# Splitting the output block of the paired units around the state

## The chip, the cores and the metric

The kernel runs on one core of a Trainium2 chip. The metric is the device time of the program in microseconds (us), measured on the chip; every launch gives one time. A profile of one launch comes with each measurement.

## The reference, cut to what matters

The reference is a retention layer (attention with a decay per head instead of a softmax) followed by a two-layer network with a squared ReLU.

```python
# q, k, v: (8, 8, 576, 64); w_in: (512, 2048); w_out: (2048, 512)
scores = scale * np.matmul(q, k.transpose(0, 1, 3, 2))
Dmat = np.where(rel >= 0, gamma[:, None, None] ** rel[None, :, :], 0.0)
attn = np.matmul(scores * Dmat, v)
x = attn.transpose(0, 2, 1, 3).reshape(4608, 512)
h = x @ w_in
g = np.maximum(h, 0.0) ** 2
out = g @ w_out
```

The decay allows the retention to be done in chunks of 128 positions. A chunk's output is a part inside the chunk (masked scores times v) plus a part from the state R, the decayed sum of k times v of all chunks before.

## The kernel before

The work is cut in 36 units (128 tokens each) in 18 groups of two. In a group, TensorE (PE) makes the scores and sums, VectorE (DVE) applies the mask and updates R, PE makes the output psO, VectorE scales it to xT, and then come the big products: ph (xT times w_in), a squared ReLU to gT, and po (gT times w_out). Groups 1 to 4 take the "paired" path, which this change is about. The other 14 groups have their own code and use a product scheme with sums such as gS and wT (VectorE sums of gT pieces and of w_out pieces).

The instructions of each engine are put in order at build time. Every task is added with an engine, a priority key, an assumed duration and its dependencies, and a small simulation of the engines pops the ready task with the lowest key. So a changed key or dependency can move other instructions too.

The paired path, with cuts marked by "...":

```python
def add_ret_pair(g):
    ...
    def fr1(s=s, src=src):     # psS + R of the unit before
        nc.vector.tensor_tensor(out=r, in0=rT["sum"][s][:, 0:256], in1=tile_of["R", src], op=ALU.add)
    def fr2(s=s, src=src):     # times the decay: the new R, two inputs from SBUF (stmp and dec)
        nc.vector.tensor_tensor(out=r..., in0=x..., in1=dec128..., op=ALU.mult)
    ...
    def inter(other):          # the part of the states, 8 small products (4 without a carried state)
        for n in range(2):
            for a, b in ((0, 0), (1, 1), (0, 1), (1, 0)):
                s = a ^ other
                if s or carry:
                    x = 2 * n + b
                    put2(s, 4 * n + 2 * a + b, tile_of["R", u + s - 1][half(a), half(x)], kqT(s)[half(a), NP + x, :], a)
    def fo():
        tile_of["psO", g] = ps_ret.tile([P, 2, 512], FP32, name="psO", tag="prO")
        inter(1)
        nc.tensor.drain()
        for m in range(NP):    # the part that needs no state, 32 small products of rx and vx
            ...
        inter(0)
    t = add("PE", base + 24, 1.3, fo, deps=masked + [T["R", u]] + ([T["R", u - 1]] if carry else []), acq=("prO",))
```

The whole output block waits for the masks and for R together. Each weight quarter is cast from a staging buffer in two halves, one on GpSimd (POOL) and one on ScalarE (ACT):

```python
def fc(eng=eng, rows=rows, sl=sl):
    (nc.gpsimd.tensor_copy if eng == "POOL" else nc.scalar.copy)(out=dst[:, rows, sl], in_=s[:, rows, sl])
```

In all later units GpSimd also multiplies v by its decay, one instruction of 128x512 per unit:

```python
def fv():
    t = tile_of["v16", u] = cast.tile([P, H, D], FP16, name="v16", tag="v16")
    nc.gpsimd.tensor_tensor(out=t, in0=tile_of["v32", u],
        in1=vdec[kind].rearrange("p (h o) -> p h o", o=1).to_broadcast([P, H, D]), op=ALU.mult)
```

Of the kernel before, what the change touches and what calls it, by code (L numbers as in the profile page):

```python
# [15 lines left out]
class Schedule:  # L16
# [7 lines left out]
    def add(self, eng, key, dur, fn, deps=(), acq=(), after=None, lag=0.0):  # L24
        t = dict(eng=eng, key=key, dur=dur, fn=fn, acq=acq, n=len(self.tasks), users=[], free=[], lag=lag,
                 left=len(deps), ready=0.0, lat=self.LAT[eng] if after is None else after)
        for d in deps:
            d["users"].append(t)
        self.tasks.append(t)
        return t  # L30
# [73 lines left out]
def kernel(  # L104
# [9 lines left out]
    nc = tc.nc  # L114
# [102 lines left out]
    for hp in range(NP):  # L217
# [18 lines left out]
                          R=6, Rm=6, kqT=6))  # L236
    add = sched.add
# [99 lines left out]
    T = {}  # L337
# [4 lines left out]
    def quad(out_, lhsT, rhs, row, col, start=True):  # L342
        nc.tensor.matmul(out_, lhsT=lhsT, rhs=rhs, start=start, stop=True, skip_group_check=True,  # L343
                         tile_position=(64 * row, 64 * col))

    def half(x):
        return slice(64 * x, 64 * x + 64)
# [90 lines left out]
    def add_ret_pair(g):  # L438

        u = groups[g][0]  # L440
        base = base_of(g)
        carry = units[u][2] > 0
        kqT = lambda s: tile_of["kqT", u + s]
        masked = []
        rT = {}
        for e in range(2):
            tag = "prS" if e == 0 else "prO"

            def fs(e=e, tag=tag):
                ps = rT["ps", e] = ps_ret.tile([P, 2, 512], FP32, name="psc", tag=tag)  # L450
                for hp in range(NP):
                    for a, s in ((0, 0), (1, 1), (0, 1), (1, 0)):
                        quad(ps[half(s), a, hp * P:(hp + 1) * P], kqT(s)[half(a), hp, half(e)], kqT(s)[half(a), NP + hp, :],
                             a, s)
            t = add("PE", base + 3 + e, 0.4, fs, deps=T["kqT", u] + T["kqT", u + 1], acq=(tag,))
            ms = []
            for a in range(2):
                def fm(e=e, a=a):
                    if a == 0:
                        rT[e] = cast.tile([P, 2, NP, P], FP16, name="rx", tag="kq16")  # L460
                    nc.vector.tensor_tensor(
                        out=rT[e][:, a], in0=rT["ps", e][:, a].rearrange("p (n i) -> p n i", i=P),
                        in1=mask2[:, e].rearrange("p (o e) i -> p o (e i)", o=1).to_broadcast([P, NP, P]), op=ALU.mult)
                ms.append(add("DVE", base + 5 + e, 0.66, fm, deps=[t] + ms, acq=() if a else ("kq",)))
            sched.free(tag, ms)
            masked += ms

        def fk():
            ps = rT["sum"] = [ps_ff.tile([P, 512], FP32, name="psS", tag="ff") for s in range(2)]
            for hp in range(NP):  # L470
                for e in range(2):
                    for s, a in ((0, 0), (1, 1), (0, 1), (1, 0)):
                        h = 4 * (hp // 2) + 2 * a + hp % 2
                        quad(ps[s][half(a), 64 * hp:64 * hp + 64], tile_of["kx", u][half(s), e, 128 * hp + 64 * a:128 * hp + 64 * a + 64],
                             tile_of["vx", u][half(s), e, 64 * h:64 * h + 64], s, a, start=hp == 0 and e == 0)
        t = add("PE", base + 4.5, 0.5, fk, deps=T["kvx", u], acq=("ff", "ff"))
        sched.free("kq", [t])
        chain = []
        for s in range(2):
            src = None if s == 0 and not carry else u + s - 1  # L480

            def fr1(s=s, src=src):
                r = tile_of["tmp", u + s] = work.tile([P, NP * D], FP32, name="stmp", tag="stmp", bufs=1)
                nc.vector.tensor_tensor(out=r, in0=rT["sum"][s][:, 0:256], in1=tile_of["R", src], op=ALU.add)

            def fr2(s=s, src=src):
                r = tile_of["R", u + s] = st_pool.tile([P, NP * D], FP16, name="R", tag="R")
                x = rT["sum"][s][:, 0:256] if src is None else tile_of["tmp", u + s]
                nc.vector.tensor_tensor(
                    out=r.rearrange("p (n d) -> p n d", d=D), in0=x.rearrange("p (n d) -> p n d", d=D),  # L490
                    in1=dec128.rearrange("p (n o) -> p n o", o=1).to_broadcast([P, NP, D]), op=ALU.mult)
            if src is not None:
                chain.append(add("DVE", base + 5.5 + s, 0.42, fr1, deps=[t] + chain[-1:] + [T["R", src]]))
                T["Rread", src].append(chain[-1])
                sched.free("ff", chain[-1:])
            chain.append(add("DVE", base + 5.6 + s, 0.5, fr2, deps=[t] + chain[-1:], acq=("R",)))
            if src is None:
                sched.free("ff", chain[-1:])
            T["R", u + s], T["Rread", u + s] = chain[-1], []

        def inter(other):
# [7 lines that stand above are left out]
        def put2(s, h, lhsT, rhs, row):  # L509
            col = h % 2  # L510
            quad(tile_of["psO", g][half(col), s, 128 * (h // 2):128 * (h // 2) + 128], lhsT, rhs, row, col,
                 start=(g, s, col) not in begun)
            begun.add((g, s, col))

        def fo():
            tile_of["psO", g] = ps_ret.tile([P, 2, 512], FP32, name="psO", tag="prO")
            inter(1)
            nc.tensor.drain()
            for m in range(NP):
                for e in range(2):  # L520
                    for s, b in ((0, 0), (1, 1), (0, 1), (1, 0)):
                        h = 2 * m + b
                        put2(s, h, tile_of["vx", u][half(s), e, 64 * h:64 * h + 64],
                             rT[e][half(s), m % 2, 2 * (m // 2) + b, :], s)
            inter(0)
        t = add("PE", base + 24, 1.3, fo, deps=masked + [T["R", u]] + ([T["R", u - 1]] if carry else []), acq=("prO",))
        for s in range(2):
            sched.free("kqT", [t])
            sched.free("kq", [t])
            if s or carry:  # L530
                T["Rread", u + s - 1].append(t)
        sched.free("kq", [t])
        for s in range(2):
            def fx(s=s):
                if s == 0:
                    tile_of["x", g] = x_pool.tile([P, NP, 2 * P], FP16, name="xT", tag="xT")
                nc.vector.tensor_tensor(
                    out=tile_of["x", g][:, :, s * P:(s + 1) * P].rearrange("p n (i e) -> p n e i", e=2),
                    in0=tile_of["psO", g][:, s].rearrange("p (n e i) -> p n e i", n=NP, e=2),
                    in1=gam_f.rearrange("p n (i e) -> p n e i", e=2), op=ALU.mult)  # L540
            T["x", u + s] = add("DVE", base + 25 + s, 0.7, fx, deps=[t] + ([T["x", u]] if s else []), acq=() if s else ("x",))
        sched.free("prO", [T["x", u + 1]])
# [7 lines left out]
    def base_of(g):  # L550
        return (units_of(g)[0] - len(groups[g])) * L - EARLY
# [168 lines left out]
    def add_ret(g):  # L720
        n = len(groups[g])
        base = base_of(g)
        if groups[g][0] < PAIRED:
            add_ret_pair(g)
            return
# [330 lines left out]
```

## Time and profile before

| | before |
|---|---|
| first three launches | 292.55, 292.39, 292.78 us |
| span of the profiled launch | 290.9 us |
| first ph | 17.27 us |
| ph goes on in group 2 | 23.09 us |
| first po that needs the last quarter of w_out ("the gate") | 38.45 us |
| first ph after group 4 | 57.20 us |
| end of the last VectorE instruction | 287.60 us |
| from there to the end of the span | 3.32 us |

All positions are from the start of the profiled span. The prediction below shows the views that these come from. In the list of the costliest groups of the kernel before, a line gives engine, operation, output and inputs, shapes and count, then the busy time in us and the mean of one in ns, then the idle time ahead of them.

```profile
L893 DVE TENSOR_TENSOR gS<-gT 128x512 f16<-128x512 f16 x64 | 30.7, 481 | 12.9 <-ACT gT L845 12.9
L367 POOL TENSOR_TENSOR v<-v,vdec_full 128x512 f16<-128x512 f32 x24 | 26.2, 1093 | 19.6 <-DMA v<-in_v_dram 14.4
```

The mean of 481 ns mixes two cases: most gS take 0.41 us, some much more. The multiply of v on GpSimd takes about 1.04 us when nothing disturbs it.

### The profile page before, as it was taken

What the parts mean: (1) busy time and instruction counts of PE and PEld (TensorE: products, weight loads), DVE (VectorE), ACT (ScalarE), POOL (GpSimd) and SP (SyncE); (2) the same over time, 40 slices, a digit from 0 to 9 for tenths busy, and PEclk for the clock granted to TensorE, in tenths of its full rate; (3) what the DMA queues carried; (4) which work ended last, traced back from release to release, by engine and by line L of the source; (5) the groups of instructions that cost most, each with busy time, mean ns of one, the idle gap of its engine ahead of it and who ended that gap; (6) DMA issues with size and microseconds to landing.
All of it is one profiled execution on the core that took longest, in us unless ns stands there. A gap on an engine that the chain in (4) does not pass through costs nothing.

```text
span 290.9 us, 10062 instructions
## 1 busy us (share of the span) xinstructions
PE 283.0 (97%) x4328; PEld 234.0 (80%) x4328; DVE 195.0 (67%) x430; ACT 187.5 (64%) x354; POOL 88.9 (31%) x123
## 2 busy tenths in 40 slices
PE   7989999999999999999999999999999999999994
PEld 2557765688888888888888888888888888888883
DVE  3796589748485848656868857667786865565632
ACT  6456966296757575867666666766767676747830
POOL 5343454524434234251616041615151400000000
PEclk9999999999999999999999999999999999999999
DMA  7999999999999899997998599979896820201004
GB/s 201 327 368 387 370 276 250 239 220 186 233 214 214 185 148 247 221 186 189 196 208 180 126 192 211 202 183 180 211 188 171 159 74 2 74 3 72 2 2 144
DMA packets 139421, 54.13 MB, mean 186 GB/s; under 512 B 118129, under 2 KB 130929, under 8 KB 139377
## 3 DMA queue, kind: packets, MB, share of 16 engines
q1 hardware_dynamic: 139072, 53.23, 81.9%
q8 instruction: 34, 0.56, 0.9%
q10 hardware_dynamic: 304, 0.26, 0.3%
q14 instruction: 11, 0.08, 0.1%
HBM read 36.70 MB, written 9.44 MB: 159 GB/s over the span
## 4 chain that ended last, share of the span: by engine, by line
PE 89%; DMA 6%; SPq 1%; issue 1%; POOL 1%; DVE 0%; DVEq 0%; POOLq 0%
PE ph L827 42%; PE po L916 34%; PE po L865 5%; PE psO L343 4%; DMA wi<-in_moe_w_in_dram 3%; DMA pair<-in_q_dram 3%; PE psc L343 2%; PE psS L343 2%; SPq L298 1%; POOL w_in L322 1%; PE psT L418 1%; DVE o L939 0%; POOL qx L403 0%; DVE p L968 0%; DVEq L939 0%
## 5 line engine op out<-in xcount | busy, mean ns | idle before, releaser
L827 PE MATMUL ph<-xT,w_in 128*128 128x256 f16 x1152 | 139.4, 273 | 0.2 <-POOL w_in L322 0.2
L827 PEld LDWEIGHTS <-w_in 128*128 128x128 f16 x1152 | 111.1, 98 | 14.8 <-POOL w_in L322 0.4
L835 ACT ACTIVATE rl<-ph 128x512 f16<-128x512 f32 x144 | 84.3, 589 | 46.9 <-PE ph L827 45.0
L845 ACT ACTIVATE gT<-rl 128x512 f16<-128x512 f16 x104 | 65.6, 631 | 3.0
L916 PEld LDWEIGHTS <-gS 128*128 128x128 f16 x512 | 49.4, 98 | 6.1 <-DVE gS L893 0.2
L916 PE MATMUL po<-wT,gS 128*128 128x256 f16 x384 | 52.4, 273 | 0.0
L893 DVE TENSOR_TENSOR gS<-gT,gS 128x512 f16<-128x512 f16 x64 | 35.1, 554 | 11.6 <-ACT gT L845 11.0
L916 PEld LDWEIGHTS <-gT 128*128 128x128 f16 x384 | 37.2, 98 | 4.4
L893 DVE TENSOR_TENSOR gS<-gT 128x512 f16<-128x512 f16 x64 | 30.7, 481 | 12.9 <-ACT gT L845 12.9
L916 PE MATMUL po<-w_out,gT 128*128 128x256 f16 x256 | 34.5, 273 | 0.0
L355 POOL CAST kq<-q 128x512 f16<-128x512 f32 x28 | 18.8, 673 | 45.7 <-DMA q<-in_q_dram 45.5
L367 POOL TENSOR_TENSOR v<-v,vdec_full 128x512 f16<-128x512 f32 x24 | 26.2, 1093 | 19.6 <-DMA v<-in_v_dram 14.4
L355 POOL CAST kq<-k 128x512 f16<-128x512 f32 x28 | 18.6, 666 | 44.4 <-DMA k<-in_k_dram 41.7
L847 DVE TENSOR_TENSOR gT<-rl 128x512 f16<-128x512 f16 x40 | 18.9, 473 | 14.7 <-ACT rl L835 14.2
L929 ACT COPY u<-po 128x256 f32<-128x256 f32 x32 | 11.8, 369 | 20.4 <-PE po L916 20.4
L939 DVE TENSOR_TENSOR o<-po,u 128x256 f32<-128x256 f32 x31 | 13.0, 421 | 16.2 <-PE po L916 8.3
L704 DVE TENSOR_TENSOR xT<-psO,gam_full 128x512 f16<-128x512 f32 x28 | 18.9, 686 | 7.5 <-PE psO L343 7.4
L643 DVE TENSOR_TENSOR rT<-psc,mask 128x512 f16<-128x512 f32 x28 | 18.3, 683 | 5.5 <-PE psc L343 5.2
L916 PE MATMUL po<-w_out,gS 128*128 128x256 f16 x128 | 17.0, 273 | 0.0
L916 PE MATMUL po<-wT,gT 128*128 128x256 f16 x128 | 16.8, 273 | 0.0
L939 DVE TENSOR_TENSOR o<-po,p 128x256 f32<-128x256 f32 x17 | 7.2, 424 | 13.7 <-ACT u L929 7.1
L865 PE MATMUL po<-w_out,gT 128*128 128x512 f16 x64 | 15.8, 380 | 0.0
(81 smaller groups left out, 244.1 us busy)
## 6 DMA issues: line engine op xcount, KB each, us to landing
out_dram<-o SPq DMA_DIRECT2D x31, 256.0 KB, 3.0
k<-in_k_dram SPq DMA_DIRECT2D x24, 256.0 KB, 4.5
q<-in_q_dram SPq DMA_DIRECT2D x24, 256.0 KB, 4.8
v<-in_v_dram SPq DMA_DIRECT2D x24, 256.0 KB, 5.3
wi<-in_moe_w_in_dram SPq DMA_DIRECT2D x4, 1024.0 KB, 10.1
wo<-in_moe_w_out_dram SPq DMA_DIRECT2D x4, 1024.0 KB, 9.7
pair<-in_k_dram SPq DMA_DIRECT2D x4, 512.0 KB, 7.0
pair<-in_q_dram SPq DMA_DIRECT2D x4, 512.0 KB, 7.0
```

Source lines behind the costliest of these rows:

```text
L343: nc.tensor.matmul(out_, lhsT=lhsT, rhs=rhs, start=start, stop=True, skip_group_check=True, tile_position=(64 * row, 64 * col))
L355: op(out=out_.rearrange("p (n b a d) -> p n b a d", n=2, b=2, a=2), in_=in_.rearrange("p (n a b) d -> p n b a d", n=2, a=2))
L367: nc.gpsimd.tensor_tensor(out=t, in0=tile_of["v32", u], in1=vdec[kind].rearrange("p (h o) -> p h o", o=1).to_broadcast([P, H, D]), op=ALU. ...
L704: nc.vector.tensor_tensor(out=tile_of["x", g][:, :, s * P:(s + 1) * P].rearrange("p n (c i) -> p c n i", c=2), in0=tile_of["psO", g][:, :, ...
L827: nc.tensor.matmul(tile_of["ph", g, fb][:, j, :], lhsT=w_in16[:, m, fi * P:(fi + 1) * P], rhs=tile_of["x", g][:, m, :], start=(m == 0), st ...
L835: nc.scalar.activation(out=t, in_=tile_of["ph", g, fb], func=ACTF.Relu)
L845: nc.scalar.activation(out=t, in_=rl, func=ACTF.Square)
L847: nc.vector.tensor_tensor(out=t, in0=rl, in1=rl, op=ALU.mult)
L865: nc.tensor.matmul(tile_of["po", u], lhsT=tile_of["g", g][:, fi, s * P:(s + 1) * P], rhs=w_out16[:, fi, :], start=(fi == 0), stop=(fi == N ...
L893: nc.vector.tensor_tensor(out=Sx(k, h), in0=in0(h), in1=in1(h), op=op)
L916: nc.tensor.matmul(tile_of["pb", g, bank], lhsT=left(i), rhs=right[:, i, :], start=(start and i == 0), stop=(i == HF - 1), skip_group_chec ...
L939: nc.vector.tensor_tensor(out=o_tile(u)[:, half * HM:(half + 1) * HM], in0=bank(x), in1=tile_of[name, g], op=ALU.add)
```

## The change

The intent: let PE do the 32 products that need no state while it would wait for R, and leave only the part of the states for after. The block becomes two tasks with a drain inside the second. The order of the parts changes from (other=1, drain, rx·vx, other=0) to (rx·vx, other=0, drain, other=1). The first line of the diff lowers the priority of R's update in the first group.

```diff
@@ -493,7 +493,7 @@
                 chain.append(add("DVE", base + 5.5 + s, 0.42, fr1, deps=[t] + chain[-1:] + [T["R", src]]))
                 T["Rread", src].append(chain[-1])
                 sched.free("ff", chain[-1:])
-            chain.append(add("DVE", base + 5.6 + s, 0.5, fr2, deps=[t] + chain[-1:], acq=("R",)))
+            chain.append(add("DVE", base + (6.5 if u == 0 else 5.6) + s, 0.5, fr2, deps=[t] + chain[-1:], acq=("R",)))
             if src is None:
                 sched.free("ff", chain[-1:])
             T["R", u + s], T["Rread", u + s] = chain[-1], []
@@ -512,18 +512,22 @@
                  start=(g, s, col) not in begun)
             begun.add((g, s, col))
 
-        def fo():
+        def fo1():
+
             tile_of["psO", g] = ps_ret.tile([P, 2, 512], FP32, name="psO", tag="prO")
-            inter(1)
-            nc.tensor.drain()
             for m in range(NP):
                 for e in range(2):
                     for s, b in ((0, 0), (1, 1), (0, 1), (1, 0)):
                         h = 2 * m + b
                         put2(s, h, tile_of["vx", u][half(s), e, 64 * h:64 * h + 64],
                              rT[e][half(s), m % 2, 2 * (m // 2) + b, :], s)
+
+        def fo2():
             inter(0)
-        t = add("PE", base + 24, 1.3, fo, deps=masked + [T["R", u]] + ([T["R", u - 1]] if carry else []), acq=("prO",))
+            nc.tensor.drain()
+            inter(1)
+        t = add("PE", base + 23.9, 0.6, fo1, deps=masked + T["kvx", u], acq=("prO",))
+        t = add("PE", base + 24, 0.75, fo2, deps=[t, T["R", u]] + ([T["R", u - 1]] if carry else []))
         for s in range(2):
             sched.free("kqT", [t])
             sched.free("kq", [t])
```

## The prediction

> **What bounds the kernel now.** I read the page first: TensorE (PE) is busy 283.0 of 290.9 us, and the chain that ended last is 89% PE.
>
> ```profile
> PE 283.0 (97%) x4328; PEld 234.0 (80%) x4328; DVE 195.0 (67%) x430; ACT 187.5 (64%) x354; POOL 88.9 (31%) x123
> ...
> PE 89%; DMA 6%; SPq 1%; issue 1%; POOL 1%; DVE 0%; DVEq 0%; POOLq 0%
> ```
>
> The Trainium skill, "Perfetto Trace Analysis", section "Optimization Strategy", says that the most contended engine may change between regimes of one kernel. The trace agrees, so the second view is the busy time by stretch; the columns are the stretch, its length, the busy time of PE, PEld, DVE, ACT and POOL with the number of instructions, PE clock, DMA share and GB/s. The last two rows are from a second, finer cut.
>
> ```profile
> 0.00:17.27 17.27, 14.95 (x202) 7.40 (x203) 10.66 (x47) 8.90 (x19) 7.51 (x25) 1.00 0.98 276
> 17.27:27.35 10.08, 8.89 (x147) 6.59 (x139) 8.00 (x14) 5.50 (x8) 4.17 (x4) 1.00 1.05 386
> 27.35:38.45 11.10, 11.06 (x89) 8.61 (x90) 5.64 (x11) 9.56 (x15) 4.53 (x4) 1.00 1.08 355
> 38.45:50.30 11.85, 11.77 (x188) 6.87 (x187) 11.21 (x19) 8.59 (x17) 5.60 (x7) 1.00 1.02 264
> ...
> 57.27:286.32 229.05, 228.68 (x3583) 200.16 (x3584) 153.07 (x328) 153.10 (x294) 62.52 (x78) 1.00 0.79 158
> ```
>
> Up to 38.45 us the DMA engines are full (shares 0.98 to 1.08, 386 GB/s at best). From 38.45 on PE is full: of the 229.05 us after 57.27 it is idle 0.37. So the time is about (when the DMA stage lets PE go) + (PE work left then) + a fixed tail. Third, the chain in order of time (start, length, what) shows where PE is let go:
>
> ```profile
> 16.14 10.06 DMA wi<-in_moe_w_in_dram
> 26.25 1.05 POOL w_in L322
> 27.35 3.23 PE ph L827 x28
> ...
> 36.66 1.75 PE ph L827 x16
> 38.45 3.18 PE po L865 x14
> ```
>
> There are two gates. The fourth quarter of w_in lands at 26.2 and is cast until 27.3: PE, which had run out of other work, starts on it at 27.35, after 0.15 us idle. The fourth quarter of w_out is the second gate. In the timeline, in order of time, it looks so:
>
> ```profile
> 36.50 1.91 PE L827 MATMUL ph<-xT,w_in 128*128 128x256 f16 x16
> 36.80 0.69 DVE L778 TENSOR_TENSOR wT<-w_out 128x1024 f16<-128x1024 f16 x1
> 37.10 1.29 POOL L322 CAST w_out<-wo 128x1024 f16<-128x1024 f32 x1 [1.74 <-DMA wo<-in_moe_w_out_dram]
> ...
> 38.45 0.81 PE L865 MATMUL po<-w_out,gT 128*128 128x512 f16 x3
> ```
>
> The ph matmuls issue every 0.109 us, so 16 from 36.50 are over at 38.25; the cast ends at 38.39 and PE goes on at 38.45. PE is 0.2 us early here. The eight weight loads are cast at 15.0, 20.6, 23.5, 26.2, 28.9, 31.6, 34.3 and 37.1: one MB each 2.7 to 2.9 us, a rate that nothing on PE touches.
>
> Last, the wait which the change is after (timeline, second of the four paired groups):
>
> ```profile
> 20.93 1.02 DVE L489 TENSOR_TENSOR R<-stmp,dec 128x256 f16<-128x256 f32 x1
> ...
> 22.00 0.31 PE L343 MATMUL psO<-kqT,R 64*64 64x128 f16 x8 [0.94 <-DVE R L489]
> ...
> 22.41 0.64 PE L343 MATMUL psO<-rx,vx 64*64 64x128 f16 x32
> 22.87 0.29 PE L343 MATMUL psO<-kqT,R 64*64 64x128 f16 x8
> 23.09 3.83 PEld L827 LDWEIGHTS <-w_in 128*128 128x128 f16 x36
> ```
>
> PE sits 0.94 us for the state R, and then has 1.09 us of output work before the next ph. All four groups lie before 57.3 us (starts 13.8, 22.0, 49.0, 56.1); the other 14 groups aren't touched.
>
> **What the skill says of it.** "TensorEngine Tiling (Array Packing)", "Gotcha 1: PSUM Pressure": different row tiles cannot access one PSUM bank at the same time, and software must synchronise. This is why there is a drain: the half of the state part called other=1 writes, from one row half of the array, the bank that the 32 rx,vx products write from the other half; other=0 writes from the same half. So the new order (rx,vx; other=0; drain; other=1) again needs exactly one drain. The trace shows it as a hole of 0.25 us before the weights of vx (22.14 to 22.40). "SBUF — State Buffer", "Who interferes with whom": VectorE operations with two SBUF inputs and GpSimd operations that read SBUF exclude one another. The trace agrees: this R (inputs stmp and dec) took 1.02 us beside the GpSimd cast of w_in at 20.63 to 21.67, against 0.42 for the next R; and the GpSimd cast at 37.10, issued beside the wT subtraction of 36.80, took 1.29 against 1.04.
>
> **The change, part by part.** Nothing is removed or added: the two programs have the same number of instructions on PE, and the same drains. What moves, by the order of instructions in the two builds:
> 1. Group 1 (first ph at 17.27). In the old order R of the first unit lay between the masks; now four masks of 0.60 us run from 10.37 to 12.8, R follows until 13.2. The rx,vx products can run at 13.0 (old: whole block at 13.78, because the transposes of qx stood before it), the state part ends at about 13.9, xT starts at 14.1 instead of 14.96: 0.9 us earlier. The price: the transposes of qx now stand behind, start at about 13.9 instead of 13.03, so ACT ends its kqT copies at 15.8 instead of 14.96 and its half of the w_in cast at 16.85 instead of 16.07. First ph near 16.6, 0.7 earlier.
> 2. Group 2. vx of the next pair still waits for its DMA at 18.03 and ends at 19.6; two masks now come behind it (old: one, plus a gT), so stmp starts at 20.8, R again runs into the GpSimd cast and ends at 21.95 as before. But the 32 rx,vx products (0.43 us of issue) are done by then. After R only 16 small products and the hole are left: 0.14 + 0.25 + 0.18 = 0.57 instead of 1.09. ph resumes at 22.6, 0.5 us earlier.
> 3. What PE does with that. In the old order 36 ph matmuls stand before the first that needs the last quarter of w_in, in the new 44. From 22.6, 16 matmuls end at 24.35, the third quarter is cast at 24.57, 28 more end at 27.7. The w_in gate is 27.3, or 27.45 where a third ReLU, now ahead of ACT's half of that cast, holds it. So PE no longer waits there and is 8 ph matmuls (0.87 us) ahead. Left before the second gate are 68 ph and 12 po: 68 x 0.109 + 12 x 0.216 = 10.0, so PE arrives at 37.7. The gate is still 38.39. It waits 0.75 instead of 0.2, and starts at 38.45 as before.
> 4. Groups 3 and 4. Masks and R were ready before PE came (R of group 3 at 47.12, its masks at 48.33, PE at 49.02), so no wait is there to remove; the same 48 or 40 matmuls and one drain are issued. Change 0.
> Sum: -0.5 to -0.9 us of PE waiting in the load stage, given back at the w_out gate; net 0, with perhaps 0.1 less from small waits after 38.45.
>
> **Rivals.** (a) The gain carries through. The 0.94 us wait and the earlier first xT speak for it; it would make 291.6 to 292.0. Against: the DMA share of 1.08 between 27.35 and 38.45, and PE early at 38.25 already. (b) The gate itself moves. If the wT subtraction no longer meets the last GpSimd cast, that takes 1.04 instead of 1.29, PE starts at 38.2: 292.3. If ACT's later first cast (0.8 us) delays the fourth w_in load, which needs that staging buffer, all later loads could slip: up to 293.3. Against: a w_in load is 10.1 us from issue to landing, so several are queued and 0.8 us of delay doesn't empty the queue. (c) More switches between 64x64 and full tiles: the same page, "Key Properties", says that changing the tiling mode drains TensorE. One warm matmul now stands between the two parts of group 2, two switches more, but inside a wait; after 38.45 the number of switches is equal. Worth nothing here.
>
> **Range and chances.** Net 0 gives 292.55; with half of the small gains 292.4. Old runs spread over 0.4 us; with (a) in part below and (b) above, 291.8 to 293.0. Two per cent is 5.9 us, more than every wait of the load stage together that the change touches, so either side has 1 to 2%.
>
> **What would show it.** Right: xT of the first group starting near 14.1; the R wait of group 2 shorter than 0.94, with ph from about 22.6; no POOL w_in wait near 27.35; po behind the ph starting at 38.4 to 38.5 with a longer hole before it, still released by a w_out cast; equal PE idle after. Wrong: po starting before 38.1 (then the gate wasn't the DMA), the loads landing later than 26.2 and 37.1, or PE after 57 us idle for more than 0.37 us by a clear margin.

## The result

| | before | after |
|---|---|---|
| median of four launches | 292.66 us | 293.07 us |
| range | 292.39 to 292.97 | 292.92 to 293.31 |

The ratio is 1.0014, with a 95% interval of 0.9997 to 1.0032: the same within 2%. Ratios in this document are the mean time of one kernel's fast runs over that of the other's of the same rounds, so they are not quite the ratio of the medians quoted. The class was predicted right and the time was not: 293.07 lies 0.07 us above the range.

The page of the changed kernel, busy time of the engines and the chain that ended last:

```profile
PE 283.4 (97%) x4328; PEld 233.9 (80%) x4328; DVE 197.9 (68%) x430; ACT 187.0 (64%) x354; POOL 89.3 (31%) x123
...
PE 83%; DMA 9%; DVE 3%; POOL 1%; SPq 1%; issue 1%; DVEq 0%; POOLq 0%
```

PE does the same 4328 instructions. DVE has a share of 3% in the chain that ended last, where it had 0% before. DVE's busy time is up by 2.9 us with the same 430 instructions, so some of them became longer. Keep that in mind.

The busy time by stretch, same cuts and columns as in the prediction:

```profile
17.27:27.35 10.08, 9.23 (x142) 6.82 (x141) 9.01 (x16) 6.00 (x9) 4.71 (x4) 1.00 1.05 385
27.35:38.45 11.10, 10.79 (x85) 8.14 (x84) 4.54 (x11) 8.87 (x15) 4.47 (x4) 1.00 1.09 357
57.27:286.32 229.05, 228.53 (x3578) 199.51 (x3576) 156.53 (x328) 153.11 (x294) 63.38 (x79) 1.00 0.77 159
```

PE has gained 0.34 us of work ahead of 27.35 (9.23 against 8.89) and has 0.27 less to do in the next stretch (10.79 against 11.06), with DMA just as full. In the long stretch it is idle 0.52 us instead of 0.37. The timeline of the load stage, lines between left out (start, length, engine, line, operation, count, and what ended an idle time):

```profile
20.58 0.42 DVE L489 TENSOR_TENSOR R<-stmp,dec 128x256 f16<-128x256 f32 x1
20.76 0.64 PE L343 MATMUL psO<-rx,vx 64*64 64x128 f16 x32
21.65 0.71 PE L343 MATMUL psO<-kqT,R 64*64 64x128 f16 x16
22.29 1.92 PE L831 MATMUL ph<-xT,w_in 128*128 128x256 f16 x16
24.54 5.41 PE L831 MATMUL ph<-xT,w_in 128*128 128x256 f16 x48 [0.33 <-POOL w_in L322]
...
36.98 1.21 POOL L322 CAST w_out<-wo 128x1024 f16<-128x1024 f32 x1 [1.71 <-DMA wo<-in_moe_w_out_dram]
38.24 3.18 PE L869 MATMUL po<-w_out,gT 128*128 128x512 f16 x14 [0.31 <-POOL w_out L322]
```

The load stage went almost as predicted. The rx·vx products now start while R is made (20.58 to 21.00), the wait of 0.94 us for R is gone, ph goes on at 22.29, PE no longer waits at 27.35, and at the gate it waits 0.31 us where it was busy until 0.2 us before it. So the gain was given back at the gate, which opened at 38.24.

Then the time was lost later. The landmarks of this launch against those of before: first ph after group 4 at 57.13 (before 57.20), so 0.07 ahead; the end of the last VectorE instruction at 288.19 (before 287.60), so 0.58 behind. No line of the change is executed in that stretch. There are places where PE falls behind, and the clearest is at 72 us:

```profile
70.88 1.04 POOL L367 TENSOR_TENSOR v<-v,vdec_full 128x512 f16<-128x512 f32 x1 [0.17 <-DMA v<-in_v_dram]
70.91 1.29 DVE L897 TENSOR_TENSOR gS<-gT 128x512 f16<-128x512 f16 x1
72.13 0.41 DVE L943 TENSOR_TENSOR o<-po,u 128x256 f32<-128x256 f32 x1
72.59 1.03 PE L920 MATMUL po<-wT,gT 128*128 128x256 f16 x8
```

GpSimd began the multiply of v at 70.88, and 0.03 us later VectorE issued a gS with both inputs in SBUF. It took 1.29 instead of 0.41 us. The o behind it, which the next po group waits for, came late. The same place in a later launch of the same kernel (run e0_after below):

```profile
70.44 0.42 DVE L897 TENSOR_TENSOR gS<-gT 128x512 f16<-128x512 f16 x1
72.26 1.04 PE L920 MATMUL po<-wT,gT 128*128 128x256 f16 x8
```

There GpSimd had started its multiply at 68.85 and ended it at 69.89, the o started at 70.98, and the po 0.33 us sooner. What differs is when the load of v landed, so this looks like chance.

These two launches are of one kernel, so PE's instructions can be set one against the other. The first launch is 0.03 us later until 72 us, 0.33 from 72.59, 0.51 from 81.81 (a gS of 1.26 us at 78.54 stands ahead, and PE's weights wait 0.29 us for a gS), and 0.71 from 149.99, where no long VectorE operation stands ahead. So two meetings made 0.48 us; the last 0.20 have another cause, which comes up again below.

My theory was therefore: **the order is worth about nothing, since the gate takes it back; the 0.4 us are scatter from meetings of VectorE and GpSimd.** The rivals: the new order costs something (in groups 3 and 4, or through the order of the accumulation), or the gate isn't the DMA and the gain was lost in another way.

### The profile page after: what moved, and what is told of

Same layout as the page of the kernel before. It is cut to its first block, busy times and chain, and to the rows that moved or that the text cites. A ratio compares the mean times of both kernels' runs of the same rounds, so it can differ in the third digit from the quotient of the medians.

```text
span 291.6 us, 10064 instructions
## 1 busy us (share of the span) xinstructions
PE 283.4 (97%) x4328; PEld 233.9 (80%) x4328; DVE 197.9 (68%) x430; ACT 187.0 (64%) x354; POOL 89.3 (31%) x123
## 4 chain that ended last, share of the span: by engine, by line
PE 83%; DMA 9%; DVE 3%; POOL 1%; SPq 1%; issue 1%; DVEq 0%; POOLq 0%
PE ph L831 38%; PE po L920 33%; PE po L869 4%; PE psO L343 4%; DMA wi<-in_moe_w_in_dram 4%; DMA wo<-in_moe_w_out_dram 3%; DMA pair<-in_q_dram 3%; PE psc L343 2%; PE psS L343 2%; SPq L298 1%; DVE gS L897 1%; POOL w_out L322 1%; PE psT L418 1%; DVE o L943 0%; DVE rT L647 0%
## 5 line engine op out<-in xcount | busy, mean ns | idle before, releaser
L897 DVE TENSOR_TENSOR gS<-gT 128x512 f16<-128x512 f16 x64 | 33.6, 526 | 12.0 <-ACT gT L849 12.0
L897 DVE TENSOR_TENSOR gS<-gT,gS 128x512 f16<-128x512 f16 x64 | 33.4, 529 | 11.8 <-ACT gT L849 11.2
L851 DVE TENSOR_TENSOR gT<-rl 128x512 f16<-128x512 f16 x40 | 21.1, 527 | 15.0 <-ACT rl L839 14.2
```

The lines of the kernel that those rows point to most:

```text
L851: nc.vector.tensor_tensor(out=t, in0=rl, in1=rl, op=ALU.mult)
L897: nc.vector.tensor_tensor(out=Sx(k, h), in0=in0(h), in1=in1(h), op=op)
```

## The experiments

Fifteen kernels ran; all gave correct results. "The stretch from 57 us" means, in the profiled launch, from the first ph after group 4 to the end of the last VectorE instruction: code that no edit of groups 1 to 4 touches.

### Both kernels again, and two partial changes

**e0_before** and **e0_after** are the two kernels unchanged, five rounds.

> The kernel before again, unchanged, against itself. All theories: ratio 1.000 within 0.1%. What is wanted is a second trace. Theory A (the loss comes after 57 us, where vector operations with two SBUF inputs meet GpSimd reads at other moments, because loads land at other moments): the pattern of long gS operations of 60 to 90 us may differ from the first trace, and with it the time by some tenths. Theory B (the loss is a fixed property of the changed order): gate at 38.4, third group's output block 1.29 us, and the late stage all repeat within 0.05 us.

> The changed kernel again, for an interval. Theory N (the 0.4 us was chance between runs): ratio 0.9995 to 1.0005. Theories A and B: 1.001 to 1.002, that is 0.3 to 0.6 us slower. In its trace A expects gS operations of over 1 us near 66, 70 and 78 us to be there again or elsewhere; B expects the third block (about 49 us) at 1.4 us again and the rest of the loss at the same places as in the first trace.

**e1_swap_in_old** keeps the schedule of before and swaps only the order inside the one block:

```diff
-            inter(1)
-            nc.tensor.drain()
             for m in range(NP): ...   # rx, vx
             inter(0)
+            nc.tensor.drain()
+            inter(1)
```

> Only the order inside the one block is changed (rx,vx; other=0; drain; other=1), everything else on every engine stands as before. My account of the prediction: the products of rx and vx run before R in group 2, ph resumes about 0.5 us earlier, the w_in gate takes it (only 36 ph stand ahead), po starts behind the ph at the same time as before within 0.1; time 292.5 to 292.7, ratio 1.000. If the new order of the block costs the loss (theory B), the block at 49 us takes 1.4 instead of 1.3 us and the ratio is 1.0005 to 1.0015. Theory A has no firm number here.

**e2_late_undone** is the changed kernel with the old block order in groups 3 and 4, inside its second task:

```diff
         def fo2():
-            inter(0)
-            nc.tensor.drain()
-            inter(1)
+            if u < 4:
+                inter(0); nc.tensor.drain(); inter(1)
+            else:                      # psO is taken here; the first task is empty
+                inter(1); nc.tensor.drain(); intra(); inter(0)
```

> The changed kernel with the old order of the block in groups 3 and 4 alone; all engines else stand as in the changed kernel. Theory B: it gets back what the block at 49 us lost (0.12 us) and, if that is what sets the later collisions, all 0.4: ratio 1.000 to 1.001. Theory A: the loads of 40 to 57 us still land as in the changed kernel, so 1.001 to 1.002 remains.

| run | median (range), five launches | ratio to before beside it, 95% interval |
|---|---|---|
| before beside them, nine launches | 292.82 (292.40 to 293.24) | |
| e0_before | 292.92 (292.55 to 293.28) | 1.0005 (0.9992 to 1.0017) |
| e0_after | 292.69 (292.62 to 293.06) | 1.0000 (0.9987 to 1.0014) |
| e1_swap_in_old | 292.74 (292.39 to 293.00) | 1.0000 (0.9988 to 1.0013) |
| e2_late_undone | 292.49 (292.40 to 292.53) | 0.9991 (0.9978 to 1.0003) |

On repetition the changed kernel equals the kernel before. The order inside the block costs nothing by itself (e1), and undoing it in groups 3 and 4 (e2) leaves the stretch from 57 us at 230.34 us, as in e0_after. The median of e2 is 0.2 us lower, and all five of its launches lie below all five of e0_after, but in the profiles this comes from the end of the program: from the last VectorE instruction to the end of the span e2 takes 3.28 us, e0_after 3.72. More of that below. The extra 0.12 us that the third paired block had taken in the first profile of the changed kernel (1.41 against 1.29 us, from 49 us on) was not there again: 1.29 in e0_after.

The profile of e0_before also corrected my picture of the wait for R. In that launch of the unchanged kernel R was quick:

```profile
20.76 0.42 DVE L489 TENSOR_TENSOR R<-stmp,dec 128x256 f16<-128x256 f32 x1
20.80 1.28 POOL L322 CAST w_in<-wi 128x1024 f16<-128x1024 f32 x1 [1.05 <-DMA wi<-in_moe_w_in_dram]
21.24 0.14 PEld L343 LDWEIGHTS <-R 64*64 64x64 f16 x8 [0.52 <-DVE R L489]
```

R started 0.04 us before the cast, took 0.42 instead of 1.02, and the cast took 1.28 in its turn. PE waited 0.52 instead of 0.94, and ph went on at 22.33, as early as in the changed kernel (22.29). This was no exception. Of the eight profiles with the schedule of before, R took 0.42 or 0.43 us in seven and ph went on between 22.10 and 22.43; the 1.02 us and 23.09 of the very first profile are the odd one. The nine profiles with the new schedule have ph going on between 22.29 and 22.73. In four of these (e4, e6, e12, e14) R did meet the cast and took 0.76 to 1.31 us, and ph still went on at 22.60 to 22.73, against 23.09 in the first profile: in such a launch the new order is worth about the 0.5 us that was predicted. So the wait that the change was made for was mostly not there to be won.

What PE does wait for in the usual launch of the kernel before is the weights. It waits once for the third and once for the fourth quarter of w_in, because only 36 ph of group 2 stand before the first that needs the fourth:

```profile
27.26 1.49 PE L827 MATMUL ph<-xT,w_in 128*128 128x256 f16 x12 [0.33 <-POOL w_in L322]
```

In the changed order there are 44, and that wait is gone. This is where the time in hand at the gate comes from.

### Is the gate the DMA, and has PE time in hand there?

**e4_after_dup4** and **e5_before_dup4** do one accumulation of four ph matmuls of group 2 twice (about 0.44 us), in the changed kernel and in the kernel before.

```diff
-                    for m in range(NP):
+                    for m in list(range(NP)) * (2 if g == 1 and fi == 8 else 1):
```

> The changed kernel with one accumulation of four ph matmuls (0.436 us, group 2, block 8, which needs no last quarter of w_out) done twice; the result is the same. Theory G (PE is early at the w_out gate by about 0.47 us in the changed kernel): po behind the ph still starts 23.2 to 23.5 us after the first w_in cast on GpSimd, with a shorter hole before it; the time is unchanged. Theory P (PE work of the load stage counts): the start moves by 0.44.

> The same four matmuls doubled in the kernel before. Theory G: PE was early by 0.2 us only, so the start of po moves by 0.44 - 0.2 = 0.24 us, to 23.6 to 23.7 us after the first w_in cast. Theory P: 0.44.

**e6_after_fine** and **e7_before_fine** cast the last quarter of w_out in four pieces of 128x512 instead of two halves, so that the first rows are ready sooner. Five rounds.

```diff
-                (nc.gpsimd.tensor_copy if ...)(out=dst[:, rows, sl], in_=s[:, rows, sl])
+                for r in (rows,) if i < 7 else (slice(j, j + 1), slice(j + 2, j + 3)):
+                    (nc.gpsimd.tensor_copy if ...)(out=dst[:, r, sl], in_=s[:, r, sl])
```

> The changed kernel, the last quarter of w_out cast in four pieces of 128x512 (GpSimd rows 0 and 2, ACT rows 1 and 3) instead of two of 128x1024; nothing else moves. Theory G: the first piece is ready about 0.65 us after the load instead of 1.2, so po starts 0.4 to 0.5 us earlier, two of its four matmuls run before the second pieces are there, and 0.43 us are won: 292.3, ratio 0.9985. Were the time not set at that gate: ratio 1.000.

> The same four pieces in the kernel before, where PE comes to the gate only 0.2 us early. Theory G: 0.2 us won, 292.6, ratio 0.9993; in the trace po starts as soon as the ph are over, without a hole. The difference to the run before this one, 0.2 us, is what the change is worth once the gate is opened.

The loads land at slightly different times in each launch, so I measure the gate from the start of the first w_in cast on GpSimd (14.74 to 15.28 us).

| run | gate after the first w_in cast | median | ratio, 95% interval |
|---|---|---|---|
| before, e0_before | 23.39, 23.44 | | |
| after, e0_after | 23.38, 23.30 | | |
| e4_after_dup4 | 23.42 | 293.61 (one launch) | |
| e5_before_dup4 | 23.64 | 292.51 (one launch) | |
| e6_after_fine | 22.59 | 292.65 (292.51 to 292.81) | 0.9991 (0.9977 to 1.0005) |
| e7_before_fine | 23.24 | 292.96 (292.57 to 293.64) | 1.0003 (0.9991 to 1.0016) |

Four more matmuls don't move the gate in the changed kernel and move it by 0.2 us in the kernel before. PE waits at this gate in the changed kernel, and the 0.44 us come out of its waiting. A finer last cast opens the gate by about 0.75 us, but only where PE is there to use it:

```profile
37.63 3.31 PE L870 MATMUL po<-w_out,gT 128*128 128x512 f16 x14
```

The po start at 37.63 instead of 38.3 (e8 and e10 below, with the same cast, have their gate at 22.80 and 22.70 of this measure). In e7 the old order has PE busy with 16 ph until just before, so it gains only 0.15 to 0.2. The gate was confirmed. The time was not (292.3 and 292.6 were expected): after 57 us the profile of e6 lost 0.43 us again in one stretch (from 88 to 103 us; a gS of 1.29 us at 94.75 stands ahead of it), and that of e4 took 0.54 us more from 57 us to the last VectorE instruction than that of e0_after (230.88 against 230.34). Of these 0.54 us, 0.35 came at 135 and 149 us with no long VectorE operation ahead. The 0.4 us that the profile of e7 lost against that of e0_before came at 149 us too. By its time alone, e4's 293.61 against the 292.69 of e0_after would have said that four matmuls cost 0.9 us. Its landmarks say otherwise.

### Double the GpSimd multiply, or halve it

**e9_before_v2x** has the kernel before do the multiply of v twice in units 8 to 21.

```diff
+            for _ in range(2 if 8 <= u < 22 else 1):
                 nc.gpsimd.tensor_tensor(out=t, in0=tile_of["v32", u], in1=vdec[kind]..., op=ALU.mult)
```

> The kernel before with GpSimd's multiply of v by its decay done twice (same result) in the units 8 to 21, all needed after 57 us; nothing before the w_out gate changes. Theory: the chance stalls of 0.1 to 0.5 us between 57 and 150 us come from VectorE operations with two SBUF inputs that meet a GpSimd operation and wait for its end. Then some 14 us more of GpSimd work make more VectorE operations long (gS above 1.2 us, against two or three of them in a run of the kernel before), the stalls between 57 and 150 us add up to 0.4 us or more, and the median rises by 0.3 to 1.5 us (ratio 1.001 to 1.005), with the gate at 23.4 us after the first w_in cast as before. Rival: the stalls have another cause (the time of the loads, PSUM buffers): gS may be longer, but the sum from the gate to the last VectorE instruction stays 249.1 to 249.6 us and the ratio 0.999 to 1.001.

**e8_late_undone_fine** has both earlier edits on the changed kernel (old order in groups 3 and 4, finer last cast). **e10_late_fine_vsplit** has those and the multiply of v in two halves:

```diff
-            nc.gpsimd.tensor_tensor(out=t, in0=tile_of["v32", u], in1=vdec[kind]..., op=ALU.mult)
+            for r in (slice(0, H // 2), slice(H // 2, H)):
+                nc.gpsimd.tensor_tensor(out=t[:, r], in0=tile_of["v32", u][:, r], in1=vdec[kind][:, r]..., op=ALU.mult)
```

> The changed kernel with both of: the old block order kept in groups 3 and 4, and the last cast of w_out in four pieces instead of two. Theory: PE has 0.3 to 0.75 us in hand before the w_out gate only with the new order in groups 1 and 2, so a finer last cast opens the gate as it did alone (22.6 us after the first w_in cast starts, against 23.4), two po wait some 0.2 us for the second pieces, and the sum is 0.4 to 0.5 us less than the kernel before in a trace free of chance stalls: last DVE end about 248.7 us after the (old) gate time. Median 292.2 to 292.5, ratio 0.998 to 0.9995. Rival 1: chance stalls of 0.1 to 0.5 us after 57 us eat it again: median 292.6 to 292.9, ratio 0.999 to 1.000. A median over 293.2 would show that the finer cast costs something elsewhere.

> As the kernel with old order in groups 3 and 4 and the finer last cast, and GpSimd's multiply of v in two halves of 128x256 in all units. Theory: a VectorE operation that meets a half waits at most some 0.55 us instead of 1.04, so gS longer than 1.2 us disappear and the chance stalls after 57 us shrink below 0.2 us in sum: median 292.1 to 292.4, and a spread of its runs below 0.4 us. Rival: the two halves follow one another so closely that VectorE waits for both, or the stalls have another cause: gS of over 1.2 us are still there and the median equals that of the kernel without the halves within 0.2 us, possibly higher by GpSimd's extra fixed cost.

| run | median (range) | ratio, 95% interval |
|---|---|---|
| before beside them, 11 launches | 292.70 (292.46 to 294.29) | |
| e9_before_v2x | 293.53 (292.38 to 293.86) | 1.0014 (0.9993 to 1.0035) |
| e8_late_undone_fine | 292.87 (292.30 to 293.25) | 0.9998 (0.9980 to 1.0016) |
| e10_late_fine_vsplit | 292.37 (292.02 to 292.55) | 0.9982 (0.9963 to 1.0000) |

Twice the multiply raised the median by 0.83 us; the interval of the ratio still includes 1, because single launches of both kernels scatter so widely (one of the kernel before took 294.29). The profile is clearer. The meeting at 72 us in e9:

```profile
70.24 2.23 POOL L368 TENSOR_TENSOR v<-v,vdec_full 128x512 f16<-128x512 f32 x2 [1.22 <-DMA v<-in_v_dram]
71.49 1.26 DVE L894 TENSOR_TENSOR gS<-gT 128x512 f16<-128x512 f16 x1
73.14 1.03 PE L917 MATMUL po<-wT,gT 128*128 128x256 f16 x8 [0.45 <-DVE o L940]
```

PE now shows the wait openly: 0.45 us for o. Set against the profile of before, PE in e9 falls 0.85 us behind between 67 and 73 us and 0.2 us between 97 and 112, each time after long operations; another 0.2 us comes at 150 us without one.

e8 met its rival 1: the earlier gate was eaten again. e10 differs from e8 in the halves alone, and is 0.5 us faster in median. Its spread, 0.53 us, was wider than the 0.4 I had expected. The profiles don't put this gain on the meetings. Their spans differ by 0.89 us. Of this, 0.42 us lies after the last VectorE instruction (3.54 us in e8, 3.12 in e10). Another 0.53 is a pause of PE in e8, at 149 us, in which the profile shows it waiting for nothing ("issue"):

```profile
148.98 0.23 PE L344 MATMUL psO<-kqT,Rm 64*64 64x64 f16 x3
149.56 0.19 PE L344 MATMUL psO<-kqT,R 64*64 64x64 f16 x1 [0.36 <-issue]
```

In e10 the same products follow without a hole. The six long gS of e8 cost it less than 0.1 us.

### The halves alone, on both orders

**e11_before_vsplit** and **e12_after_vsplit** are the two kernels with the multiply of v in halves (the diff of e10) and nothing else. **e13_before_vsplit_again** and **e14_after_vsplit_again** are the same two once more, because e12 had gained more than the theory said.

> The kernel before with GpSimd's multiply of v in two halves of 128x256 in all units, nothing else. Theory: what scatters the times of one kernel by 0.4 us and more is VectorE's two-input operations waiting for the end of this multiply; halves take most of that away. Then no single gS or R takes 1.14 us or more between 57 and 150 us, from the gate to the last VectorE instruction it is 249.0 to 249.2 us, the gate is where it was (23.2 to 23.5 us after the first w_in cast), the median is 292.3 to 292.7 and the runs lie within 0.5 us. Rival: the low median with halves came from the finer last cast alone: then this kernel equals the kernel before within 0.1 us in median, with as wide a spread.

> The changed kernel with GpSimd's multiply of v in two halves, nothing else. Theory: with the chance stalls mostly gone the change alone is seen more sharply: net 0, so the median is within 0.15 us of that of the kernel before with halves (292.3 to 292.7), and its profile has no single gS or R of 1.14 us or more between 57 and 150 us. Rival: the changed order does cost something that the stalls had hidden or carried (the 293.07 of its first record): median 0.3 us or more above that of the kernel before with halves.

> The kernel before with the multiply of v in halves, once more. Theory: what the record of the changed order with halves gained over it (292.11 against 292.56 us) is at most 0.1 to 0.2 us of earlier gate, and the rest is scatter of five runs: the median is 292.4 to 292.7. Gate 23.2 to 23.5 us after the first w_in cast, from the gate to the last VectorE instruction 249.0 to 249.3 us.

> The changed kernel with the multiply of v in halves, once more, beside the kernel before with halves on the same chip. Theory: net 0 to -0.2 us: PE comes to the w_out gate with 0.3 to 0.5 us in hand, so it starts with the cast whenever the load lands early, which the old order can use only for its 0.1 to 0.2 us in hand; median 292.2 to 292.5, within 0.25 us of the other. Rival: once the late stalls are small the changed order does gain: again 0.35 us or more below the other, with the gate under 23.1 us after the first w_in cast. If it comes out above the other, the first pair was scatter alone.

| run | median (range) | ratio to before, 95% interval | gate after the first w_in cast |
|---|---|---|---|
| before beside them, 10 launches | 292.79 (292.52 to 293.23) | | |
| e11_before_vsplit | 292.56 (292.22 to 292.83) | 0.9992 (0.9979 to 1.0006) | 23.39 |
| e13_before_vsplit_again | 292.32 (292.21 to 292.69) | 0.9986 (0.9973 to 0.9998) | 23.40 |
| e12_after_vsplit | 292.11 (291.89 to 292.36) | 0.9977 (0.9964 to 0.9989) | 23.05 |
| e14_after_vsplit_again | 292.09 (291.98 to 292.39) | 0.9977 (0.9963 to 0.9991) | 23.25 |

The ten launches beside e13 and e14 are the nine beside e11 and e12 (median 292.69) and one more. e11 was nearer to its rival than to the theory: its median is 0.13 us below the nine, and its spread of 0.61 us is wider than the 0.5 I had expected (theirs was 0.71). The median of e13 came out below the range I gave.

A gS that meets a half waits less: no gS or R after 57 us took over 0.88 us in e10 to e14. The place at 70 us again, in e11:

```profile
70.49 1.44 POOL L368 TENSOR_TENSOR v<-v,vdec_full 128x256 f16<-128x256 f32 x2 [1.27 <-DMA v<-in_v_dram]
70.62 0.84 DVE L894 TENSOR_TENSOR gS<-gT 128x512 f16<-128x512 f16 x1
72.45 1.04 PE L917 MATMUL po<-wT,gT 128*128 128x256 f16 x8
```

The meeting is there, 0.84 us long, but the po directly follows the eight matmuls ahead of it (71.56 to about 72.43). The halves cost GpSimd time (two of 0.68 against one of 1.09 us); PE shows no wait for it.

But this isn't where the profiles with halves gained. From 57 us to the last VectorE instruction e11 and e13 took 230.44 and 230.36 us, before and e0_before 230.40 and 230.49; e12 and e14 took 230.34 and 230.33, e0_after and e2 230.34 and 230.34. What is shorter is the end, from the last VectorE instruction to the end of the span: 2.95 to 3.12 us in the five profiles with halves, 3.28 to 3.72 in the eleven with the multiply whole. Neither VectorE nor GpSimd computes anything there, and e9, with more GpSimd work instead of less, has 3.00. So the lower medians of e10 to e14 are not shown to come from fewer meetings. Why the end differs between kernels stays open.

With the halves in both, the changed order is faster. The nine launches of e12 and e14 have a mean of 292.13 and the eleven of e11 and e13 a mean of 292.47: 0.34 us less, with a standard error of 0.09 from the scatter of the launches, ratio 0.9988. The first pair alone (0.45 us in the medians) was more than my theory had and less than it looked; the second pair (0.23 us) lay inside the 0.25 I allowed, though its own median was below the range I gave. The rival of e14, 0.35 us or more and a gate under 23.1, was not met either.

Part of the gain is at the gate. The last cast and what runs beside it, e13 (old order) and then e14 (new order):

```profile
36.88 0.68 DVE L779 TENSOR_TENSOR wT<-w_out 128x1024 f16<-128x1024 f16 x1
37.20 1.26 POOL L322 CAST w_out<-wo 128x1024 f16<-128x1024 f32 x1 [1.70 <-DMA wo<-in_moe_w_out_dram]
38.52 1.67 PE L866 MATMUL po<-w_out,gT 128*128 128x512 f16 x7
```

```profile
36.73 0.68 DVE L783 TENSOR_TENSOR wT<-w_out 128x1024 f16<-128x1024 f16 x1
37.10 1.22 POOL L322 CAST w_out<-wo 128x1024 f16<-128x1024 f32 x1 [1.69 <-DMA wo<-in_moe_w_out_dram]
38.37 1.89 PE L870 MATMUL po<-w_out,gT 128*128 128x512 f16 x8 [0.30 <-POOL w_out L322]
```

In the new order the squares gT, and with them the wT subtraction, come some 0.15 us earlier, so the subtraction gets out of the way of the GpSimd cast sooner. In the four profiles of the old order without edits in the load stage that I compared (before, e0_before, e11, e13) that cast took 1.29, 1.30, 1.31 and 1.26 us (e9: 1.30). In those of the new (after, e0_after, e2, e12, e14) it took 1.21, 1.22, 1.22, 1.24 and 1.22. The means are 1.29 and 1.22, so this is worth 0.07 us. In all of them, and in e1 (1.21) and e4 (1.38), the cast ends 1.58 to 1.59 us after the wT subtraction starts. The gates of e12 and e14 open at 38.33 and 38.37, those of e11 and e13 both at 38.52: 0.17 us. The spans of the four profiled launches (290.8 and 290.6 against 290.4 and 290.4) differ by 0.3 us in the mean: 0.17 at the gate, 0.07 lost after it in the old order (0.10 in e11, nearly all of it at the pause of 149 us, 0.03 in e13), and 0.07 in the end of the program (3.03 against 2.96 us). Only the 0.07 us of the cast have a cause that I can show. Whether the loads land a little earlier with the new order or did so by chance stays open, and two profiles of each kernel can't tell.

Without the halves the end works against the change: at the last VectorE instruction e0_after is 0.17 us ahead of e0_before (287.44 against 287.61), and at the end of the span 0.27 us behind.

e12 and e14 are the fastest versions that ran, 0.6 to 0.7 us below the kernel before in median, with intervals that exclude 1. In the profiles 0.34 us of this is the shorter end (2.96 against 3.30).

### All profiles side by side

Long is the number of single gS or R of over 1.0 us between 57 and 150 us (multiplies of v go on until 230 us, and some later gS are long too). The block at 149 us is the time from the first psS product there to the next ph. The end runs from the last VectorE instruction to the end of the span. Times in us.

| profile | order | multiply of v | long | stretch from 57 us | block at 149 us | end |
|---|---|---|---|---|---|---|
| before, e0_before | old | whole | 2, 2 | 230.40, 230.49 | 0.76, 0.91 | 3.32, 3.28 |
| e1, e5, e7 | old, edited | whole | 1, 6, 4 | 230.34, 230.37, 230.86 | 0.76, 0.76, 1.28 | 3.54, 3.29, 3.41 |
| after, e0_after | new | whole | 6, 2 | 231.05, 230.34 | 0.95, 0.76 | 3.41, 3.72 |
| e2, e4, e6, e8 | new, edited | whole | 2, 4, 5, 6 | 230.34, 230.88, 230.78, 230.99 | 0.76, 0.95, 0.76, 1.32 | 3.28, 3.71, 3.35, 3.54 |
| e9 | old | twice | 9 | 231.67 | 0.97 | 3.00 |
| e11, e13 | old | halves | 0, 0 | 230.44, 230.36 | 0.85, 0.79 | 3.09, 2.98 |
| e10, e12, e14 | new | halves | 0, 0, 0 | 230.49, 230.34, 230.33 | 0.76, 0.76, 0.76 | 3.12, 2.97, 2.95 |

The stretch has a floor of 230.33 us. All profiles with at most two long operations are within 0.16 us of it; with four or more, six of seven are 0.45 to 1.34 us above it. The exception is e5, with six and no loss: a long gS only costs if its consumer has no slack. The count alone misleads, though. The block at 149 us takes 0.76 us at best and up to 1.32, and nearly all that e7 and e8 lost is there; the long operations account for the losses of e6 and e9 and for about 0.5 us of that of the first profile of the changed kernel. What holds PE in that block the profiles don't show. In this table the new order with a whole multiply has more long operations than the old (six, two, two, four, five and six against two, two, one, six and four). With so few profiles I can't say whether it provokes them.

## Why the prediction was right or wrong

**The net was right in class, and the reason for it.** That the gate takes PE's gain back is shown by e4 to e7: PE gets there early, more work is free there, and a finer cast lets the gain through.

**Step 1 (group 1).** xT at 14.10 as predicted; first ph at 16.85 to 17.01 in the changed kernel, a gain of 0.1 to 0.4 where 0.7 was said (measured from the first w_in cast, 0.2 in every profile).

**Step 2 (group 2).** ph went on at 22.29, predicted 22.6. But the step also said that "R again runs into the GpSimd cast", and that the old order would go on at 23.09. R took 0.42 us, and the old order goes on at 22.10 to 22.43 in seven profiles of eight. A single profile had shown the rarer outcome of a meeting that 0.04 us decide, and the predicted gain of 0.5 us is about 0.

**Step 3 (the gate).** The 44 ph in place of 36 do remove the wait for the fourth quarter of w_in, and PE's arrival near 37.7 was right: 12 ph from 36.46 at 0.109 us. It waited less than the 0.75 us of the prediction, 0.31 us for PE and 0.48 for its weight loads, since the gate came earlier. The gate itself was put at 38.45 "as before". It opened at 38.24 and 38.34 in the first two profiles; with the halves the new order has it 0.17 us earlier than the old. (A slip without effect: of the eight weight loads only the last seven are 2.7 to 2.9 us apart; between the first two lie 5.6 us.) The small side of rival (b), the wT subtraction meeting the last cast less, did happen: 0.07 us of it instead of 0.25.

**Step 4 (groups 3 and 4).** Change 0, as e1 and the repeated profile show; e2 leaves the stretch after 57 us as it was.

**Rivals (a) and (c).** The gain did not carry through: no launch of the changed kernel without other edits was below 292.62. No run singles out the mode switches of (c).

**The step that failed is the sum behind the range.** The prediction took the time as the gate plus "(PE work left then) + a fixed tail", and allowed for the rest only that "old runs spread over 0.4 us". The gate held: 38.24 against 38.45. The other two terms are not fixed. From 57 us to the last VectorE instruction the changed kernel took 231.05 us in the launch that was profiled first and 230.34 in the second; the tail behind it took 3.41 and 3.72 us, against 3.32 in the kernel before. And "0.4 us" read three launches as the scatter of the kernel. Launches of the unchanged kernel lie between 292.39 and 294.29, and medians of four or five launches of one kernel differ by as much as 0.4 us: the changed kernel gave 293.07 and 292.69. The term was mis-sized: 0.4 us is not the width of the scatter but what a whole median can move by. Added to both ends, it gives a range of 291.4 to 293.4, by hindsight. The prediction named the test that the first profile failed ("PE after 57 us idle for more than 0.37 us by a clear margin"), but put no width on it, and counted only causes inside the change.

The runs showed one cause outside it: VectorE's two-input operations meeting GpSimd's multiply of v and its casts, in a part that the change doesn't touch. In the first profile two such meetings made 0.48 of the 0.71 us between 231.05 and 230.34, and doubling the multiply (e9) brought nine long operations, about 1 us of PE falling behind after them, and a median 0.83 us higher. A second cause, the pause at 149 us, made 0.20; what causes it is open. That the other three launches of that first set, which have no profile, were slow for the same reasons is likely but not shown.

That the change gains 0.34 us with the halves in was not predicted; half of that is seen at the gate, and most of its cause remains open.

## What to carry to other kernels

Before giving a narrow range, find out how far launches of one kernel scatter and which stage makes the scatter; three launches don't tell. When a profile is slower in a stretch that the edit doesn't touch, compare it by landmarks with a second profile of the same kernel before explaining it. Cutting a long GpSimd instruction shortens the wait of a VectorE operation that meets it (0.84 instead of 1.29 us here), but a lower median doesn't prove that this is the reason: here the halves left the stretch with the meetings as it was in undisturbed launches, and the gain showed at the end of the program. Compare every stretch, the end too, before naming a cause.

## What the Trainium skill lacked or had wrong

- "SBUF — State Buffer", "Who interferes with whom", says that issue order decides which of VectorE and GpSimd blocks. The runs agree: gS 1.29 against 0.41 us when issued 0.03 us after GpSimd's multiply; R 0.42 us when 0.04 us ahead of the cast, which then took 1.28 against 1.04. What the page lacks is that this order changes from launch to launch of one kernel where GpSimd waits for loads: at the same place of one kernel gS took 1.29 us in one launch and 0.42 in another, and PE was 0.30 us later for it.
- The same page doesn't name shorter GpSimd instructions as a remedy: with GpSimd's instruction in two halves the operation that meets it takes 0.84 us instead of 1.29, at a price of 0.26 us more on GpSimd (2 x 0.68 against 1.09).
- "TensorEngine Tiling (Array Packing)" asks for synchronisation between row tiles on one PSUM bank, and gives no cost for it. Where the drain stands there is a hole of 0.25 us in the kernel before ("[0.25 <-issue]" ahead of the weights of vx in e0_before too).
